# A first batch split by halves of j over all four pieces, and q = 0 copies on ScalarE, in a Fourier-mixing and MLP kernel

## The chip, the cores and the metric

The kernel runs on one core of a Trainium2 chip. The core has five engines, each with its own stream of instructions in a fixed order: TensorE (PE in the profile, with its weight loads listed apart as PEld), VectorE (DVE), ScalarE (ACT), GpSimd (POOL) and SyncE (SP, which only issues DMAs). Instructions on different engines wait for each other through semaphores. DMAs move data between DRAM and the on-chip memory SBUF; matmul results stand in a small memory called PSUM, from which ACT and DVE read.

The metric is the device time of one execution in microseconds (us), less is better. Times are medians of several executions. The profile is of one execution of its own.

## What is computed

The input is `x` of 8 x 4224 x 192 (batch, position, channel), a table of 8 x 7 taps, and two weight matrices. First comes a causal depthwise convolution over positions, with taps that went through a softmax; each of 8 groups of 24 channels has its own 7 taps. Then the real part of a two-dimensional Fourier transform over positions and channels is added to the signal, the sum is normalised, goes through a two-layer MLP, and is added again:

```python
w = np.exp(w); w = w / (np.sum(w, axis=-1, keepdims=True) + 1e-09)
out = np.einsum('hk,bskhg->bshg', w, x_unf)            # 7 taps, 8 groups
...
X = np.fft.fft(np.fft.fft(x, axis=1), axis=2)
u = x + np.real(X).astype(np.float32)
un = (u - mu) / np.sqrt(var + 1e-06)
ch = np.maximum(un @ w_ch1, 0.0) @ w_ch2               # 192 -> 768 -> 192
return (u + ch).astype(np.float32)
```

## The kernel before

**Stages of one batch.** Numbers with L are line numbers.

- *conv.* `conv_unit` loads nothing itself: windows of x (`xt`, from `load_windows`) are multiplied with a band matrix of taps on PE (L387), copied to `xa`, and stored to a scratch in DRAM, `sc`. Six chunks to a batch.
- *load and split.* `load_x` reads the rows back from `sc` in another layout, in four pieces of the index b (`PIECES`: 9, 8, 8 and 8 wide), into `xs` tiles. `split_x` writes each value as a sum of two float16 numbers, so that float16 matmuls keep nearly float32 accuracy: ACT writes the high part `XH` (L472), DVE the remainder `XL` (L473). A piece is split in two halves of b, so there are eight calls of each to a batch.
- *stage A.* `stage_a` has 16 tiles, each with some of the indices j, which go over the short transforms' columns. A tile's matmuls (L490) read the columns of XH and XL for its own j, and all b. The PSUM tile `pa` is split again: ACT writes `yh` (L498), DVE `yl` (L499).
- *stage B.* `stage_b` runs 8 times to a batch (L516 on PE, then ACT L524 and DVE L525 write `V`). At the end of each, POOL copies the q = 0 part of `V` to `V0` (L531), 2 x 6 x 8 values to a partition. V0 is read only by the ninth iteration of the batch, called `Q0`.
- *iterations.* Eight iterations of 512 positions each, and Q0 with 128. For each, POOL gathers the convolved rows into `xr` with indirect DMAs (`load_res`, L544, four to an iteration). `prep` does the last transform on PE (`pq`, L574), ACT moves it to `u` (L591), POOL adds `xr` (L592), DVE takes the statistics, small operations on ACT, DVE and POOL follow, then the normalised rows `un` (DVE or ACT, L623 and L628), and their two float16 parts in `hl` (ACT L638, POOL L641). `transposes` turns `hl` into `kt` with a transposing DMA on SP (L651). `mlp_hidden` (PE `ph` L680, ACT `hh` L684, DVE `hlo` L685) and `mlp_out` (PE `po` L699 to L705, DVE L711) are the MLP; then `u` is stored.

**Order.** The source is written in the order of priority. The scheduler of the language simulates the engines and orders each engine's instructions from that, and an `issue_after(...)` holds an instruction back in that order until another one has been issued. A tile with a `tag` takes one of the `bufs` buffers of that tag; a new tile waits for all readers of the one that had its buffer. Tags are shared between purposes whose lives do not overlap. In the first batch, `xs` pieces 0 and 1 are in the tag `xs` and pieces 2 and 3 in `yh` and `yl`, and the raw words of the second weight matrix (`raw_w2`, two tiles) are in `hlo`, which later holds the low part of the hidden layer.

**The start.** The first batch has nothing to run beside it. It is written out by hand before the main loop: windows, conv, `scales`, four `load_x`, eight `split_x` (L819 to L822), the conversion of the MLP's weights, 16 `stage_a`, then the gathers of iterations 0 and 1, two `stage_b`, the preparation of these two iterations at high priority, then the gathers of iterations 2 and 3 behind `lower[0]`, the last POOL instruction that writes `hl` of iteration 1, then the conv of batch 1 and the rest of the first stage B:

```python
    with tc.issue_after(lower[0]):
        for f in gathers(2) + gathers(3):
            f()
```

In the main loop, which has one turn to an iteration, the preparation of iterations 2 to 4 ahead and the conv, split and stages of the next batch are spread between the MLP's matmuls. There `split_x(bt, i)` is called with i from 0 to 7 at places set by `split_at` and `split_1`: two calls, then the loads, then the others.

## Time and profile before

| | us |
|---|---|
| median of the runs (3) | 1337.24 |
| lowest and highest of them | 1334.99, 1337.45 |
| the profiled execution, its own time | 1339.74 |
| span of that execution's profile | 1338.0 |
| busy time of POOL's gathers, L544, 264 of them | 283.0 |
| busy time of PE in `ph`, L680, 2160 matmuls | 504.0 |
| idle time of PE before L699, put down to ACT `hh` | 34.1 |

The mean granted clock of TensorE over the span was 0.96 of full speed. A busy time is the sum of the durations of an engine's instructions. An idle time before a group of instructions is given with the instruction that ended it, written `<-ACT hh L684`. `<-issue` is idle time in which the engine waited for nothing that the profile shows, and `<-remote` a wait that ended with an event of a queue or a core that it cannot name. In a timeline row stand start, duration, engine, line, operation, output<-inputs, shapes, and how many like it follow; in a row of windows the window, its length, and the busy time with the number of instructions for PE, PEld, DVE, ACT and POOL, then clock, DMA share and GB/s.

### The profile page before, as it was taken

The numbers are of one execution on the slowest core, as the hardware profiler recorded it, in microseconds if no ns is written. First come the engines' busy times: TensorE is split into PE (matmuls) and PEld (weight loads), VectorE is DVE, ScalarE is ACT, GpSimd is POOL, SyncE is SP. The second block draws the span as 40 slices with busy tenths as digits, with TensorE's granted clock in tenths as the row PEclk, the third lists the DMA queues.
The fourth block names the chain that finished last, engine by engine and source line by source line (L and its number), as shares of the span: only waits on it lengthen the run. The fifth ranks groups of instructions, "written<-read, shape, count | busy, mean of one in ns | idle before, by whom it ended". The sixth has DMA issues, their size and how long they took to land.

```text
span 1338.0 us, 30108 instructions
## 1 busy us (share of the span) xinstructions
PE 1204.8 (90%) x12224; PEld 943.1 (70%) x12224; DVE 745.0 (56%) x1635; ACT 819.0 (61%) x1562; POOL 666.5 (50%) x1052
## 2 busy tenths in 40 slices
PE   4186689998999989998999989999889998999999
PEld 4175458885777767786778857777567876777767
DVE  7763365456545565456644575446654566555443
ACT  4643387558755686557865586556755667545642
POOL 0236535457445664457444574456634576456520
PEclk9588889998999999999999999999899999999999
DMA  8934395556555566456554576555564444223321
GB/s 274 241 90 125 90 246 142 104 132 166 132 124 128 126 149 144 121 129 167 120 139 103 122 178 127 128 125 129 141 137 108 116 96 95 69 63 84 75 63 39
DMA packets 225819, 170.19 MB, mean 127 GB/s; under 512 B 119560, under 2 KB 207440, under 8 KB 225680
## 3 DMA queue, kind: packets, MB, share of 16 engines
q1 hardware_dynamic: 163408, 108.53, 35.4%
q10 hardware_dynamic: 49600, 33.77, 10.0%
q0 software_dynamic: 12672, 25.97, 7.5%
q8 instruction: 95, 1.56, 0.5%
q14 instruction: 44, 0.36, 0.1%
HBM read 83.73 MB, written 58.55 MB: 106 GB/s over the span
## 4 chain that ended last, share of the span: by engine, by line
PE 35%; POOL 24%; issue 17%; ACT 11%; DVE 5%; DMA 4%; another core or an unknown queue 1%; SPq 1%; ACTq 0%; POOLq 0%; DVEq 0%
PE ph L680 12%; POOL xr L544 11%; PE pa L490 5%; ACT un L628 4%; POOL u L592 4%; PE po L699 4%; PE po L705 4%; PE po L702 4%; POOL hl L641 4%; DMA xs<-sc 3%; PE pc L387 3%; DVE XL L473 2%; PE pq L574 2%; ACT hl L638 2%; ACT hh L684 1%
## 5 line engine op out<-in xcount | busy, mean ns | idle before, releaser
L680 PE MATMUL ph<-kt,W 128*128 128x512 f16 (+1 forms) x2160 | 504.0, 367 | 18.5 <-DMA kt<-hl 8.4
L685 DVE SCALAR_TENSOR_TENSOR hlo<-ph,hh 128x512 f16<-128x512 f32 (+1 forms) x400 | 270.8, 679 | 346.5 <-ACT hh L684 342.0
L699 PE MATMUL po<-W,hh 128*128 128x192 f16 x1584 | 387.9, 248 | 45.7 <-ACT hh L684 34.1
L702 PE MATMUL po<-W,hh 128*128 128x192 f16 x1584 | 387.9, 248 | 1.3 <-issue 1.3
L705 PE MATMUL po<-W,hlo 128*128 128x192 f16 x1584 | 384.1, 247 | 1.8 <-issue 1.5
L684 ACT ACTIVATE hh<-ph 128x512 f16<-128x512 f32 (+1 forms) x400 | 236.5, 593 | 199.2 <-PE ph L680 141.3
L544 POOL DMA_INDIRECT xr<-sc,rows_sb x264 | 283.0, 1072 | 134.4 <-issue 60.7
L680 PEld LDWEIGHTS <-W 128*128 128x128 f16 x2160 | 196.4, 99 | 170.7 <-issue 25.7
L641 POOL TENSOR_TENSOR hl<-un,hl 128x512 f16<-128x512 f32 (+1 forms) x144 | 129.4, 920 | 219.0 <-ACT hl L638 210.4
L699 PEld LDWEIGHTS <-hh 128*128 128x128 f16 x1584 | 155.8, 98 | 58.9 <-ACT hh L684 38.6
L592 POOL TENSOR_TENSOR u<-u,xr 128x768 f32<-128x768 f32 (+1 forms) x72 | 121.1, 1682 | 129.9 <-ACT u L591 129.7
L702 PEld LDWEIGHTS <-hh 128*128 128x128 f16 x1584 | 155.8, 98 | 28.7 <-issue 14.1
L705 PEld LDWEIGHTS <-hlo 128*128 128x128 f16 x1584 | 155.6, 98 | 27.5 <-issue 5.8
L628 ACT ACTIVATE un<-u,nm,y 128x192 f32<-128x192 f32 x256 | 120.2, 539 | 53.9 <-POOL nm L618 49.5
L387 PE MATMUL pc<-xt,band 128*120 128x144 f32 x756 | 120.5, 301 | 24.2 <-DMA band<-line_d 15.0
L387 PEld LDWEIGHTS pc<-xt,band 128*120 128x120 f32 x756 | 107.3, 193 | 32.6 <-issue 16.1
L490 PE MATMUL pa<-c_sb,XH 128*128 128x128 f16 x1024 | 103.2, 223 | 22.2 <-ACT XH L472 19.1
L711 DVE SCALAR_TENSOR_TENSOR u<-po,fo,u 128x384 f32<-128x384 f32 (+1 forms) x136 | 81.4, 599 | 62.1 <-PE po L705 46.7
L473 DVE SCALAR_TENSOR_TENSOR XL<-xs,s_x,XH 128x768 f16<-128x768 f32 x64 | 104.2, 1638 | 17.1 <-ACT XH L472 10.3
L499 DVE SCALAR_TENSOR_TENSOR yl<-pa,yh 99x512 f16<-99x512 f32 x128 | 85.3, 682 | 49.1 <-ACT yh L498 45.7
L472 ACT ACTIVATE XH<-xs,s_x 128x768 f16<-128x768 f32 x64 | 106.3, 1694 | 7.9 <-DMA xs<-sc 7.9
L490 PEld LDWEIGHTS <-XH 128*128 128x128 f16 x1024 | 82.6, 99 | 32.6 <-ACT XH L472 19.7
(125 smaller groups left out, 1461.5 us busy)
## 6 DMA issues: line engine op xcount, KB each, us to landing
out_dram<-u SPq DMA_DIRECT2D x64, 384.0 KB
xt<-in_xw_dram SPq DMA_DIRECT2D x42, 576.0 KB
sc<-xa ACTq DMA_DIRECT2D x42, 540.0 KB
xs<-sc SPq DMA_DIRECT2D x96, 192.0 KB
xs<-sc SPq DMA_DIRECT2D x32, 216.0 KB
xr<-sc,rows_sb POOLq DMA_INDIRECT x264
sc<-xa ACTq DMA_DIRECT2D x7, 450.0 KB
xt<-in_xv_dram SPq DMA_DIRECT2D x6, 504.0 KB
```

What stands on the lines that cost most here:

```text
L387: nc.tensor.matmul(pc[:WR, h - h0], band[:, h, :WR], xt[:, :, h * GRP : (h + 1) * GRP], start=True, stop=True,)
L490: nc.tensor.matmul(pa[:, i], x[:, at], F[:, l], start=(n == 0), stop=(n == 2))
L544: nc.gpsimd.indirect_dma_start(bt.xr[it][:, g], None, bt.sc[:S], bass.IndirectOffsetOnAxis(ap=rows_sb[:, col : col + 1], axis=0),)
L592: nc.gpsimd.tensor_tensor(u[:, :ng], u[:, :ng], xr[:, :ng], op=ALU.add)
L628: nc.scalar.activation(un[:, g], u[:, g], AF.Identity, bias=nm[:, g : g + 1], scale=y[:, g : g + 1],)
L641: lower[0] = nc.gpsimd.tensor_tensor(bl[:, :, o : o + n], un[:, :ng, f], hi[:, :, f], op=ALU.subtract).ins
L680: nc.tensor.matmul(ph[:, n], W1[:, w, ht * 128 : (ht + 1) * 128], kt[:, k], start=(i == 0), stop=(i == len(order) - 1),)
L684: anchor[0] = nc.scalar.activation(hh, ph, AF.Relu).ins
L685: nc.vector.scalar_tensor_tensor(hlo, ph, 0.0, hh, op0=ALU.max, op1=ALU.subtract)
L699: nc.tensor.matmul(po[:, g % 2], hh[:, ht, tk], W2[:, ht, 0], start=(ht == 0), stop=False)
L702: nc.tensor.matmul(po[:, g % 2], hh[:, ht, tk], W2[:, ht, 1], start=False, stop=False)
L705: nc.tensor.matmul(po[:, g % 2], hlo[:, ht, tk], W2[:, ht, 0], start=False, stop=(ht == 5),)
```

## The change

There are five edits; what is computed stays the same.

1. **Split by j.** `split_x` takes half of the j of a whole piece (9 or 8 wide in b), where it took all j of half a piece. For the first batch, the first halves of all four pieces come first, then the second halves. In later batches the calls keep their places, so the two halves of one piece follow each other.
2. **Slots at the start.** Pieces 2 and 3 of the first batch's `xs` go to the tag `hlo` instead of `yh` and `yl`, and the raw words of the second weight matrix to `xa` instead of `hlo`.
3. **Copies of q = 0.** The copy from `V` to `V0` is an activation on ACT instead of a copy on POOL.
4. **Buffers.** `xr` has 4 buffers instead of 3 and `un` 2 instead of 1.
5. **Gathers at the start.** Those of iterations 2 and 3 follow those of 0 and 1 directly; the `issue_after(lower[0])` goes.

```diff
-        tag, bufs = (("yh", 1), ("yl", 1))[i - 2] if b == 0 and i > 1 else ("xs", 2)
-        xs = sb.tile([NA, 9, D], F32, tag=tag, name=f"xs_{b}_{i}", bufs=bufs)
+        tag, bufs, n = ("hlo", 2, 8) if b == 0 and i > 1 else ("xs", 2, 9)
+        xs = sb.tile([NA, n, D], F32, tag=tag, name=f"xs_{b}_{i}", bufs=bufs)
...
-                raw(f"w2_{i}", "hlo")[:, : 6 * D].rearrange("p (c e) -> p c e", c=3),
+                raw(f"w2_{i}", "xa", 3 * D)[:, : 6 * D].rearrange("p (c e) -> p c e", c=3),
...
-        first = PIECES[i][0]
-        b0, b1 = ((first, first + 4), (first + 4, PIECES[i][1]))[half]
-        src = bt.xs[i][:, b0 - first : b1 - first].rearrange("p b (t j) -> p j (b t)", t=ND)
+        b0, b1 = PIECES[i]
+        js = slice(half * NJ // 2, (half + 1) * NJ // 2)
+        src = bt.xs[i][:, : b1 - b0].rearrange("p b (t j) -> p j (b t)", t=ND)[:, js]
...
-                :, :, ND * b0 : ND * b1
+                :, js, ND * b0 : ND * b1
...
-    for i in range(2 * NPC):
-        split_x(first, i)
+    for half in range(2):
+        for i in range(NPC):
+            split_x(first, 2 * i + half)
...
-        nc.gpsimd.tensor_copy(
+        nc.scalar.activation(
             bt.V0.rearrange("p l m c -> p (l m) c")[:, :, it * CG : (it + 1) * CG],
             V.rearrange("p l (m q) c -> p (l m) q c", q=NQ)[:, :, 0],
+            AF.Copy,
         )
...
-            bt.xr[it] = sb.tile([128, 4, D], F32, tag="xr", name=f"xr_{b}_{it}", bufs=3)
+            bt.xr[it] = sb.tile([128, 4, D], F32, tag="xr", name=f"xr_{b}_{it}", bufs=4)
...
-        un = sb.tile([128, 4, D], F32, tag="un", name=f"un_{b}_{it}", bufs=1)
+        un = sb.tile([128, 4, D], F32, tag="un", name=f"un_{b}_{it}", bufs=2)
...
-    for f in gathers(0) + gathers(1):
+    for f in gathers(0) + gathers(1) + gathers(2) + gathers(3):
         f()
...
-    with tc.issue_after(lower[0]):
-        for f in gathers(2) + gathers(3):
-            f()
```

More of the change, by code (lines that the diff above doesn't have):

```diff
@@ L37 @@
 PIECES = ((0, 9), (9, 17), (17, 25), (25, 33))
+NPC = len(PIECES)
 DUP = 9 * WR
@@ L227, in tmp @@
         def tmp(i):
-            t = sb.tile([128, HID], F32, tag=("kt", "hl", "un")[i], name=f"cv{i}_{name}", bufs=(3, 2, 1)[i])
+            t = sb.tile([128, HID], F32, tag=("kt", "hl", "un")[i], name=f"cv{i}_{name}", bufs=(3, 2, 2)[i])
             return t[:rows, :n]
@@ L249, with raw @@
     raws = {}
-    def raw(name, tag):
-        raws[name] = sb.tile([128, HID, 2], I32, tag=tag, name=f"raw_{name}")
+    def raw(name, tag, n=HID):
+        raws[name] = sb.tile([128, n, 2], I32, tag=tag, name=f"raw_{name}")
         return raws[name].rearrange("p n t -> p (n t)")
@@ L733 @@
     NT = NJ // JT
-    NPC = len(PIECES)
     NIT = NPAIR + 1
```

## The prediction

> **What bounds the kernel now.** I began with the page: span, busy line and the row of the granted clock.
>
> ```profile
> span 1338.0 us, 30108 instructions
> PE 1204.8 (90%) x12224; PEld 943.1 (70%) x12224; DVE 745.0 (56%) x1635; ACT 819.0 (61%) x1562; POOL 666.5 (50%) x1052
> PEclk9588889998999999999999999999899999999999
> ```
>
> TensorE (PE) is 90% busy and no other engine is over 61%. The clock is below full in the first slices only, so the start differs from the rest. The view of windows shows by how much (columns: window, its length, busy time and instructions of PE, PEld, DVE, ACT, POOL, clock, DMA share, GB/s):
>
> ```profile
> 0.00:60.00 60.00, 16.22 (x102) 15.77 (x102) 43.74 (x100) 30.45 (x47) 2.90 (x6) 0.79 0.95 274
> 60.00:100.00 40.00, 32.11 (x378) 30.19 (x379) 28.18 (x62) 23.00 (x43) 15.88 (x27) 0.80 0.33 93
> 100.00:124.00 24.00, 13.32 (x144) 9.70 (x142) 7.43 (x15) 8.11 (x16) 15.32 (x21) 0.78 0.58 150
> 124.00:160.00 36.00, 31.08 (x263) 24.36 (x262) 17.68 (x55) 12.40 (x29) 20.87 (x37) 0.87 0.26 74
> 160.00:180.00 20.00, 8.97 (x37) 5.48 (x38) 6.70 (x6) 14.48 (x19) 7.37 (x6) 0.77 0.91 210
> 200.00:1338.00 1138.00, 1084.98 (x11137) 843.76 (x11134) 627.18 (x1377) 712.03 (x1382) 598.43 (x948) 0.99 0.51 118
> ```
>
> From 200 us on PE is busy 1085.0 of 1138 us: it is the bound, and only 53 us are idle. Before, it idles 10.7 us in 100 to 124 (24 less 13.32), 4.9 in 124 to 160 and 11.0 in 160 to 180. Work that PE can start earlier there ends the program earlier, one for one. Nearly all of the change acts there; only the copies for q = 0 act in every batch. Three rows of PE's timeline show what it waits for:
>
> ```profile
> 61.64 1.03 PE L490 MATMUL pa<-c_sb,XH 128*128 128x128 f16 x8 [18.48 <-ACT XH L472]
> 123.32 0.34 PE L699 MATMUL po<-W,hh 128*128 128x192 f16 x1 [7.15 <-ACT hh L684]
> 166.89 4.33 PE L680 MATMUL ph<-kt,W 128*128 128x512 f16 x10 [8.09 <-DMA kt<-hl]
> ```
>
> These are stage A waiting for the split, the second matmul of iteration 0 waiting for ACT, and iteration 2, whose transposed input arrives late.
>
> **The split by halves of j.** Rows of ACT and DVE around stage A of the first batch:
>
> ```profile
> 48.58 3.55 ACT L472 ACTIVATE XH<-xs,s_x 128x768 f16<-128x768 f32 x2 [6.25 <-DMA xs<-sc]
> 52.13 9.46 ACT L472 ACTIVATE XH<-xs,s_x 128x768 f16<-128x768 f32 x6
> 62.83 1.15 ACT L343 ACTIVATE sq<-xt 128x1152 bf16<-128x1152 f32 x1
> 60.35 2.95 DVE L473 SCALAR_TENSOR_TENSOR XL<-xs,s_x,XH 128x768 f16<-128x768 f32 x2
> 63.24 1.52 DVE L313 SCALAR_TENSOR_TENSOR W<-w,s_w,W 128x576 f16<-128x576 f32 x2
> 65.87 0.69 DVE L499 SCALAR_TENSOR_TENSOR yl<-pa,yh 99x512 f16<-99x512 f32 x1 [1.11 <-ACT yh L498]
> 70.93 7.69 DVE L499 SCALAR_TENSOR_TENSOR yl<-pa,yh 99x512 f16<-99x512 f32 x12 [0.51 <-ACT yh L498]
> ```
>
> Two rows of all later splits say that the cost goes by elements:
>
> ```profile
> L472 ACT ACTIVATE XH<-xs,s_x 128x768 f16<-128x768 f32 x42 | 68.0, 1645 | 0.0
> L472 ACT ACTIVATE XH<-xs,s_x 128x960 f16<-128x960 f32 x6 | 12.2, 2031 | 0.0
> ```
>
> 1645/768 and 2031/960 are both 2.1 ns. Halves of 864 for the first piece and 768 for the others have the same sum as now, so the splits cost nothing more, in later batches too. What changes is that four splits, not eight, release seven of the sixteen tiles of stage A: PE can start near 57 us, not 63. But the four `pa` buffers let it run only four tiles ahead, and ACT and DVE still have the other four splits and W2 before the first `yh` and `yl`. DVE is free at 63.24 + 1.52 = 64.8 us; sixteen `yl` of 0.64 (7.69/12) then end at 75.0 where they end at 78.6 now: 3.6 us at best. ACT has sixteen `yh` and four squares of 1.35 (L343 and its read) in the same stretch, some 13.7 us from 62.8: 76.6 and a gain of 2.0. I take **2.5 us**. That pieces 2 and 3 go to `hlo` frees `yh` and `yl` for this start. Two windows of batch 1 that reuse `xs` now wait for both halves of pieces 0 and 1, some 3 us more; they are used after 88 us, which hides it.
>
> The lower end is in the w2 loads. They move from `hlo` to `xa` slots, so to after the stores of `xa`, beside the loads of `xs`.
>
> ```profile
> raw_w<-in_w_dram ACTq DMA_DIRECT2D x2, 576.0 KB
> DMA packets 5563, 4.07 MB, mean 255 GB/s; under 512 B 270, under 2 KB 5562, under 8 KB 5562
> ```
>
> The second row is the window 34 to 50 us, where 255 GB/s is all that is moved. 1152 KB there are up to 4.6 us in which `xs` could come later. Against that, the same bytes leave the time ahead of the stores, where the DMA share is 0.95 too, so the stores end earlier; I take nothing, bound +4.6. DVE's conversions of w2 fall into its gap of 6.85 us before the first XL.
>
> The Trainium skill (TensorE: Matmul & The Clock Gate, Part 1: The HAM clock gate) says that after an idle window of about 3.4 us the array is back at half rate. By that rule PE, starting at 57 and then waiting for the first `yl`, would run the next 3.4 us at half rate, and the 2.5 would be 0.8. No run here shows this order yet.
>
> **Gathers 2 and 3 and the copies leave POOL's path.** POOL's rows:
>
> ```profile
> 68.40 0.95 POOL L544 DMA_INDIRECT xr<-sc,rows_sb  x1 [0.31 <-issue]
> 104.84 1.08 POOL L544 DMA_INDIRECT xr<-sc,rows_sb  x1
> 118.90 0.95 POOL L544 DMA_INDIRECT xr<-sc,rows_sb  x1 [0.31 <-issue]
> 123.45 0.27 POOL L531 COPY V<-V 128x96 f16<-128x96 f16 x1 [3.12 <-DVE V L525]
> 123.68 1.81 POOL L592 TENSOR_TENSOR u<-u,xr 128x768 f32<-128x768 f32 x1
> 103.10 1.22 ACT L591 ACTIVATE u<-pq,g 128x384 f32<-128x384 f32 x3 [0.29 <-PE pq L574]
> ```
>
> `u` of iteration 2 is ready from ACT at 104.3 us, but POOL adds `xr` at 123.68: before it stand twelve gathers (104.84 to 119.85) and four copies, the last of which waits for V. After the change eight of the gathers follow the first eight directly: 69.4 plus 8 x 1.25 (issue to issue) is 79.4 us. The adds of iterations 0 and 1, which start at 83.64 now and near 81 then, stay clear of them by 1.7 us, and DMA share in 60 to 100 is 0.33. The addition for iteration 2 can come near 106. Its statistics, `un` and transpose follow, and the 8.09 us in which PE waits for its `kt` go; these I count whole, **8 us**. What is late next is the window that conv waits for at 176.93; that 4.1 us wait stays in the sum. With `un` doubled, this row's wait (and one like it at 167.75) goes too:
>
> ```profile
> 163.12 1.86 ACT L628 ACTIVATE un<-u,nm,y 128x192 f32<-128x192 f32 x4 [1.89 <-POOL hl L641]
> ```
>
> It lies in the same late chain, so it adds nothing. Bounds: 0 (something else is late) to 12.2.
>
> **The stall of 108 to 122 us.**
>
> ```profile
> 113.81 0.51 ACT L524 ACTIVATE V<-pb 128x408 f16<-128x408 f32 x1 [5.34 <-remote]
> 122.26 0.51 ACT L524 ACTIVATE V<-pb 128x408 f16<-128x408 f32 x1 [7.95 <-remote]
> 122.81 0.58 DVE L525 SCALAR_TENSOR_TENSOR V<-pb,V 128x408 f16<-128x408 f32 x1 [7.88 <-ACT V L524]
> ```
>
> ACT waits 13.3 us for something the trace cannot name, PE idles 10.7, and both waits lie inside the run of twelve gathers. A run of eight, 57 to 69.4, had no such stall. So I know the place and not the cause. If the stall goes with the eight gathers of twelve, it is 7.1 us; I take half, **3.5 us**. Bounds: 10.7 gained, or 7.1 lost if it goes with them into stage A.
>
> **The clock.** Two waits of PE that should shrink (before 123 and before 166.9) are followed by slow rows:
>
> ```profile
> 124.00:126.00 2.00, 2.00 (x10) 2.00 (x10) 1.04 (x2) 2.00 (x5) 1.49 (x1) 0.50 0.01 4
> 168.00:170.00 2.00, 2.00 (x6) 0.75 (x5) 0.00 (x0) 2.00 (x5) 0.00 (x0) 0.50 1.08 203
> ```
>
> Some 4 us at half rate after each are 2 us lost each. I count one: **2 us** (0 to 4).
>
> **The copies on ACT.** The operation is not in the trace on ACT; the nearest rows bound it.
>
> ```profile
> L531 POOL COPY V<-V 128x96 f16<-128x96 f16 x64 | 17.9, 281 | 94.6 <-DVE V L525 94.5
> L610 ACT ACTIVATE sd<-mv,eps 128x4 f32<-128x4 f32 x64 | 19.0, 296 | 57.7 <-DVE mv L599 52.4 <-DVE hlo L685 3.5 <-issue 1.1
> L638 ACT ACTIVATE hl<-un 128x192 f16<-128x192 f32 x8 | 2.9, 361 | 0.2
> PE po L699 <- ACT hh L684: 26.4, 19, 2.9
> ```
>
> 4 columns take 296 ns and 192 take 361, so 96 take some 0.33 us. Fifty-six of the 64 lie after 200 us. A copy must also wait for DVE's V: ACT ends its half at 122.77, DVE at 123.39, so ACT stands up to 0.62 us unless other work is put between. At most 0.95 us each, 53 in all. Behind a waiting copy stand `hh` (L684) on ACT, and PE's `po` behind that. The last row counts that wait from 200 us on: 19 times, among 379 `hh` activations, 5%. By that share 53 us of ACT cost PE 2.7; with copies put where V is already there, 18.5 us cost 0.9. I take **2 us lost**. Upper end: ACT is busy 712 of 1138 us, 63%, and if PE lost that share of 53 it would be 33. POOL loses 64 x 0.28 us of work and 94.5 us of waiting, but after 200 us PE waits for no `kt`, so that gains nothing; below zero I allow 1.
>
> **Sum.** -2.5 - 8 - 3.5 - 2 + 2 = -14. The profiled execution took 1339.74 us (span 1338.0 and 1.7 around it), 2.5 over the median of the runs, 1337.24. With the median as base: **1323 us**.
>
> **Rivals.**
> - *The stall goes along* (0.18). Sixteen gathers in one run, 57 to 79.4, stand beside the whole of stage A. For: both long waits lie in such runs. Against: the first run of eight. Where the stall only moves, stage A's 2.5 is lost with it: 1337.2 - 8 - 2 + 2 = 1329; where it also grows by its 7.1 there, 1336. I take 1330.
> - *xs comes later* (0.10). The w2 loads delay the first split by 4.6 us: 1328. Beside it: the Trainium skill (DMA: Bandwidth & Descriptors, Queues, rings and completion order) has each engine take turns between the queues it has work for; by that rule w2 on ACT's queue would take a share from `xs` on SP's, which speaks against this part of the change.
> - *Nothing is left of it* (0.11). Iteration 2 comes earlier, but PE then waits where it is idle next, for batch 1's windows and `xs`, DMA-bound at a share of 0.91 in 160 to 180 us: only stage A and what the copies cost remain, 1337. That is also what is left if the halves don't release PE, as four `pa` buffers allow little.
> - *ACT becomes late* (0.16), the other side. Each copy holds ACT until DVE's V, `hh` comes late, PE idles. With the start gaining 16, it decides from 16/56 = 0.29 us of PE per copy. Half of the bound, 0.5 us each, is 28 us: 1349; at the bound of 33, 1354.
> - The forecast, 1323, has 0.45.
>
> **How the numbers follow.** All gains at their ends (3.6, 12.2, 10.7, 4, 1) would give 1306. The range leaves out the last of that and most of the case in which ACT is late: 1309 to 1343. About 0.2% is what a measurement of this kernel can tell from no change (1334.6 to 1339.9). Faster: 0.45, nearly all of the first two rivals (0.24) and a little of the third: 0.72. Same: most of the third and the edge of the first: 0.12. Slower: the last, 0.16.
>
> **What would show it.** Stage A: the first `pa` matmul with XL near 57 us and the last `yl` near 76. Gathers: sixteen between 57 and 80 us, and the add for iteration 2 near 106. PE: the window 160 to 180 busy 17 us or more, not 9. The stall: no wait of ACT's V over 2 us. ACT: the wait of `po` for `hh` from 200 us on still near 26 us. I am wrong if that wait is over 40, if the stall stands at another place with its full length, or if the hole before iteration 2 only moves.

## The result and the profile after

The changed kernel takes **1346.17 us** (median of 5 runs, 1342.87 to 1348.13). The kernel before takes 1337.45 us on the same chip (5 runs). The ratio is **1.0061**, 95% interval 1.004 to 1.0081: slower by 0.6%. The forecast was 1323 us, with a range up to 1343.

The page of the changed kernel, whose profiled execution took 1348.13 us (span, busy line, granted clock):

```profile
span 1346.2 us, 30076 instructions
PE 1209.6 (90%) x12224; PEld 944.1 (70%) x12224; DVE 746.0 (55%) x1635; ACT 830.3 (62%) x1626; POOL 641.5 (48%) x988
PEclk9577899998999989999899989999999998999999
```

POOL has 25 us less work and ACT 11 more, but PE is busy 4.8 us longer for the same 12224 matmuls, and the span is 8.2 us longer. The view of windows (columns as before) shows the start:

```profile
60.00:100.00 40.00, 25.70 (x292) 22.12 (x293) 21.00 (x37) 21.27 (x41) 17.38 (x17) 0.71 0.27 89
100.00:124.00 24.00, 16.41 (x142) 15.44 (x141) 13.86 (x41) 7.06 (x17) 17.20 (x29) 0.72 0.64 177
124.00:160.00 36.00, 28.85 (x271) 21.89 (x269) 18.70 (x57) 20.51 (x46) 20.88 (x32) 0.93 0.79 176
160.00:180.00 20.00, 17.40 (x147) 13.88 (x146) 10.54 (x12) 16.10 (x25) 4.62 (x8) 0.95 1.02 221
200.00:1346.20 1146.20, 1089.19 (x11122) 844.38 (x11119) 625.08 (x1373) 720.78 (x1432) 570.58 (x886) 0.98 0.50 117
```

The hole of 160 to 180 us is gone: PE is busy 17.4 there, not 9. But 86 matmuls are missing from 60 to 100 us. One mark helps to divide the program: the start of the n-th hidden activation (`hh`, one to each group of `ph`, 50 to a batch), read from the trace of both kernels. All numbers in this table are such starts, counted from the first instruction.

| `hh` number | before, us | changed, us | difference |
|---|---|---|---|
| 0 | 106.3 | 126.2 | +19.9 |
| 12 | 169.5 | 171.2 | +1.7 |
| 48 (end of batch 0) | 284.0 | 282.4 | -1.6 |
| 99 | 441.1 | 442.5 | +1.3 |
| 249 | 907.1 | 914.6 | +7.6 |
| 399 (last) | 1330.2 | 1338.5 | +8.2 |

So there are **two results, not one**. The start gains 1.6 us, where 16 were forecast. And from `hh` 48 on the changed kernel loses 9.8 us, where the copies were forecast to cost 2. Inside a batch the loss stands at one place: in each batch from the second to the fifth the difference grows by 1.9 to 2.8 us, nearly all of it between the hidden units 4 and 22, mostly in iterations 1 and 2. Behind them it departs by up to 1.2 us at single units and comes back.

For the start, rows of ACT, DVE and POOL in the timeline of the changed kernel:

```profile
72.46 0.60 ACT L499 ACTIVATE yh<-pa 99x512 f16<-99x512 f32 x1 [1.81 <-PE pa L491]
83.78 0.60 ACT L499 ACTIVATE yh<-pa 99x512 f16<-99x512 f32 x1 [10.73 <-remote]
90.38 3.67 DVE L500 SCALAR_TENSOR_TENSOR yl<-pa,yh 99x512 f16<-99x512 f32 x6
81.53 0.94 POOL L546 DMA_INDIRECT xr<-sc,rows_sb  x1 [0.30 <-issue]
99.43 1.81 POOL L594 TENSOR_TENSOR u<-u,xr 128x768 f32<-128x768 f32 x1 [16.96 <-ACT u L593]
113.81 0.21 POOL L617 TENSOR_TENSOR t<-t,w 128x4 f32<-128x4 f32 x1
123.80 1.81 POOL L594 TENSOR_TENSOR u<-u,xr 128x768 f32<-128x768 f32 x1 [1.05 <-ACT u L593]
```

The wait that the trace cannot name (the stall), seen before at 108 to 122 us, now stands in stage A: 10.7 us of ACT before 83.78, beside the run of sixteen gathers that ends at 82.5. The last `yl` ends at 94.1, not 76. Then the addition for iteration 0 (99.43) and a later small step of its chain on POOL (`t`, L617, 113.81) lie 14 us apart, because eight more gathers, of iterations 4 and 5, went between them (101.5 to 113.8): the fourth `xr` buffer let them through. The addition for iteration 2, which was to move from 123.7 to 106, stays at 123.8; it waits there for `u` from ACT.

### The profile page after: what moved, and what is told of

Same layout as the page of the kernel before. It is cut to its first block, busy times and chain, and to the rows that moved or that the text cites. A ratio compares the mean times of both kernels' runs of the same rounds, so it can differ in the third digit from the quotient of the medians.

```text
span 1346.2 us, 30076 instructions
## 1 busy us (share of the span) xinstructions
PE 1209.6 (90%) x12224; PEld 944.1 (70%) x12224; DVE 746.0 (55%) x1635; ACT 830.3 (62%) x1626; POOL 641.5 (48%) x988
## 4 chain that ended last, share of the span: by engine, by line
PE 38%; POOL 18%; issue 15%; ACT 10%; DMA 9%; DVE 6%; SPq 1%; ACTq 1%; POOLq 0%; DVEq 0%
PE ph L682 14%; POOL xr L546 9%; PE po L707 4%; PE po L701 4%; PE po L704 4%; POOL u L594 4%; PE pa L491 4%; ACT un L630 4%; DMA out_dram<-u 3%; PE pc L388 3%; PE pq L576 3%; POOL hl L643 2%; ACT hh L686 2%; DVE XL L474 2%; DMA xs<-sc 2%
## 5 line engine op out<-in xcount | busy, mean ns | idle before, releaser
L546 POOL DMA_INDIRECT xr<-sc,rows_sb x264 | 278.8, 1056 | 138.5 <-DMA xt<-in_xw_dram 60.7
L704 PEld LDWEIGHTS <-hh 128*128 128x128 f16 x1584 | 155.8, 98 | 21.4 <-issue 6.8
L491 PE MATMUL pa<-c_sb,XH 128*128 128x128 f16 x1024 | 109.6, 227 | 39.8 <-ACT XH L473 29.2
L388 PE MATMUL pc<-xt,band 128*120 128x144 f32 x756 | 118.2, 297 | 28.2 <-DMA band<-line_d 14.9
L388 PEld LDWEIGHTS pc<-xt,band 128*120 128x120 f32 x756 | 105.7, 190 | 38.4 <-issue 16.7
L491 PEld LDWEIGHTS <-XH 128*128 128x128 f16 x1024 | 85.4, 101 | 51.2 <-ACT XH L473 29.3
L474 DVE SCALAR_TENSOR_TENSOR XL<-xs,s_x,XH 128x768 f16<-128x768 f32 (+1 forms) x64 | 101.2, 1590 | 25.1 <-ACT XH L473 24.9
L499 ACT ACTIVATE yh<-pa 99x512 f16<-99x512 f32 x128 | 74.7, 599 | 64.7 <-PE pa L491 25.1
```

The lines of the kernel that those rows point to most:

```text
L388: nc.tensor.matmul(pc[:WR, h - h0], band[:, h, :WR], xt[:, :, h * GRP : (h + 1) * GRP], start=True, stop=True,)
L491: nc.tensor.matmul(pa[:, i], x[:, at], F[:, l], start=(n == 0), stop=(n == 2))
L546: nc.gpsimd.indirect_dma_start(bt.xr[it][:, g], None, bt.sc[:S], bass.IndirectOffsetOnAxis(ap=rows_sb[:, col : col + 1], axis=0),)
L704: nc.tensor.matmul(po[:, g % 2], hh[:, ht, tk], W2[:, ht, 1], start=False, stop=False)
```

## The experiments

A ratio is against the kernel before on the same chip, with its 95% interval. The series ran on more than one chip: the kernel before took 1337 to 1339 us in the first three series and 1314 in the last two, so only ratios compare across them. Where a batch's length is given, it is the mean distance from `hh` 50n to `hh` 50(n+1) over the second to the fifth batch, in the one profiled execution; for the kernel before it is 155.3 us, for the changed one 157.6.

### Each part undone

Copies back on POOL:

```diff
-        nc.scalar.activation(V0 slice, V slice, AF.Copy)
+        nc.gpsimd.tensor_copy(V0 slice, V slice)
```

> The changed kernel with the q = 0 copies back on GpSimd, all else as changed. From 210 us to the end the changed kernel loses 10.4 us on the kernel before (its 24th hh is 2.6 us earlier, its last 7.9 later). Copies theory: these 10 us are ACT waiting for DVE's V at the copies, so this run takes 1336 us, 10 below the changed kernel. Buffers theory (second un) and split theory (halves of j): the copies cost the 2 us that I forecast, 1344. Either way the first hh stays near 126 us.

Measured: 1330.91 us, 0.9956 (0.9943 to 0.997). This is faster than both kernels, by 15 us against the changed one. A batch takes 155.3 us again. The first `hh` stays at 126.1. In the profiles it beats the kernel before by 4.7 us up to `hh` 48 and by 4.0 after it, and the 4.0 come from one batch that is not in the means: `hh` 250 to 300 takes 158.1 us here, 163.0 before and 162.4 in the changed kernel.

The halves of b again, in every batch:

```diff
-        b0, b1 = PIECES[i]
-        js = slice(half * NJ // 2, (half + 1) * NJ // 2)
+        first = PIECES[i][0]
+        b0, b1 = ((first, first + 4), (first + 4, PIECES[i][1]))[half]
...
-    for half in range(2):
-        for i in range(NPC):
-            split_x(first, 2 * i + half)
+    for i in range(2 * NPC):
+        split_x(first, i)
```

> The changed kernel with the split by halves of b again, in every batch and in the old order for the first; slots, copies, buffers and gathers stay as changed. The loss of each later batch, 2.0 to 2.4 us, falls in its iterations 1 and 2, where the next batch is split. Split theory: that loss goes with the halves of j, 1336 us. Buffers and copies theories: 1346 within 2, and the loss per batch stays. At the start the halves of j released stage A at 60.6 us where it was 61.6, so undoing them costs 1 us at most.

Measured: 1356.83 us, 1.0143 (1.0125 to 1.0161). The split theory falls: undoing the halves of j does not remove the loss of the later batches (158.6 us each). It costs 10.7 us, so beside the other edits the halves of j are worth that much, about half of it at the start (`hh` 48 at 287.3 instead of 282.4) and 1.0 us in each later batch.

One `un` buffer (the temporary of the weights' conversion that has the same tag goes back to one with it):

```diff
-        un = sb.tile([128, 4, D], F32, tag="un", name=f"un_{b}_{it}", bufs=2)
+        un = sb.tile([128, 4, D], F32, tag="un", name=f"un_{b}_{it}", bufs=1)
```

> The changed kernel with one un buffer instead of two (and one of the conversion's temporaries with it), all else as changed. Buffers theory: with two, ACT takes the four un of an iteration ahead of an hh and then stands waiting for POOL's nm (3.1 us at 471.8 to 474.8 us of the changed kernel, hh behind it, PE idle 2.1), so the 10 us go: 1336. Copies and split theories: 1346, or up to 3 more for the waits of un that come back.

Measured: 1341.53 us, 1.0033 (1.002 to 1.0046). A batch takes 156.3 us, between the two. The second buffer does harm here, but it doesn't make up the whole loss.

Gathers of iterations 2 and 3 late again:

```diff
-    for f in gathers(0) + gathers(1) + gathers(2) + gathers(3):
+    for f in gathers(0) + gathers(1):
         f()
...
+    with tc.issue_after(lower[0]):
+        for f in gathers(2) + gathers(3):
+            f()
```

> The changed kernel with the gathers of iterations 2 and 3 behind the last hl of iteration 1 again, all else as changed. Theory of the moved stall: the run of sixteen gathers, 61 to 82.5 us, is what holds PE in stage A at one instruction in 0.7 us from 69.2 to 84.9; with eight gathers the yl end near 80 and the first hh comes near 107 instead of 126. The hole before iteration 2 returns (8 us), so the time is within 4 us of the changed kernel's 1346. Rival: stage A is slow for another reason (W2's conversion on DVE, four pa buffers): the gaps of 1.0 to 1.15 us in stage A stay, and the first hh stays past 120.

Measured: 1362.43 us, 1.0191 (1.0175 to 1.0206). In stage A the theory of the moved stall held: with eight gathers (60 to 73 us) only 2.5 us of waits without a name are left there, and the last `yl` ends at 84.1. The first `hh` comes 9.6 us earlier, at 116.6, but not near 107, as the first transpose took 12.4 us from issue. The time was far off the 1346 within 4 us. With four `xr` buffers the late gathers run into those of iterations 4 and 5, a run of sixteen from 105.9 to 125.9 us with 10.3 us of that wait in it, and `hh` 48 comes 17.5 us later than in the changed kernel. The early gathers are worth that.

### The copies and the second buffer

Copies on POOL and one `un` buffer; and the kernel before with nothing but the copies on ACT:

> Copies back on GpSimd and one un buffer. With the copies on ACT one buffer was 4.6 us faster than two (1341.5 against 1346.2). If the second buffer by itself lets un stand ahead of hh on ACT, the same comes off again: 1326. If it only did harm together with the copies, 1331 within 2, or slower by the waits of un on hl (1.9 us each at 163 and 168 us of the kernel before).

> The kernel before with the q = 0 copies on ACT and nothing else of the change. Copies theory: they cost 15.3 us in the changed kernel (1346.2 less 1330.9), spread over the batches at 1.8 each, whatever else is there: 1352 within 4. Rival, an interaction with two un buffers: 1340 or less, about the 2 us that I forecast. Rival, chance of the order that the scheduler finds: no even slope, but steps at single iterations.

Measured: 1337.99 us, 0.9986 (0.9973 to 1.0), and 1339.41 us, 0.9999 (0.9987 to 1.0011). In both the main theory was wrong and a rival held, and together they say what the first four runs could not. The copies alone cost nothing in the time. Beside the rest of the change they cost 0.5% with one buffer (1.0033 against 0.9986) and 1.05% with two (1.0061 against 0.9956), and the second buffer without them is a gain of 0.3%. The lengths of a batch show the same:

| a batch, us | one `un` | two `un` |
|---|---|---|
| copies on POOL | 156.0 | 155.3 |
| copies on ACT | 156.3 | 157.6 |
| copies on ACT, in the kernel before | 155.8 | |

With one buffer a batch loses 0.3 us by the copies (0.5 in the kernel before, which is within the spread of its four batches, 155.1 to 156.4). With two it loses 2.3. The groups of ACT in the changed kernel and in the kernel before with the copies alone (times busy, mean, idle before it):

```profile
L532 ACT ACTIVATE V<-V 128x96 f16<-128x96 f16 x64 | 17.9, 280 | 16.5 <-DVE V L526 15.9 <-DVE XL L474 0.5
```

```profile
L531 ACT ACTIVATE V<-V 128x96 f16<-128x96 f16 x64 | 18.0, 282 | 17.5 <-DVE V L525 17.5
```

The 64 copies hold ACT for 34 to 36 us in both. In the first they make a batch 2.3 us longer, in the second 0.5. So the price isn't in the time that ACT gives to them.

To see which copies do it, they were divided:

```diff
+        if it < 5:      # and, in the second run, it >= 5
+            nc.scalar.activation(to, q0, AF.Copy)
+        else:
+            nc.gpsimd.tensor_copy(to, q0)
```

> The changed kernel with the copies of stage B 0 to 4 on ACT and those of 5 to 7 on POOL. In the changed kernel the loss of each batch falls in its iterations 1 and 2 (hidden units 6 to 18), the copies of stage B 0 to 4 of the next batch fall elsewhere, and there no hh moves by more than 0.2 us. Theory: the loss hangs on what stands on ACT and POOL at iterations 1 and 2, so without those three copies it goes whole: 0.994 to 0.998 of the kernel before, as with all copies on POOL (0.9956). Rival, an even price of each copy (15 us over 64): 5.7 us less than the changed kernel, 1.002. Rival, a chance order: no rule, anywhere from 0.995 to 1.008.

> The other way round: copies of stage B 5 to 7 on ACT, 0 to 4 on POOL. Theory: the whole loss stays, 1.006 of the kernel before with 2.0 to 2.4 us lost in iterations 1 and 2 of each batch. Rival, an even price: 9.5 us less than the changed kernel, 0.999. Rival, a chance order: anywhere from 0.995 to 1.008, and then this run and the one with 0 to 4 do not add up to the changed kernel.

Measured: 1336.22 us, 1.0001 (0.9986 to 1.0015), with a batch of 155.1 us; and 1350.6 us, 1.0095 (1.0077 to 1.0113), with a batch of 157.4. In the batches the theory held: the loss hangs on the three copies of stage B 5 to 7, which fall in iterations 0 and 1, and the other five cost nothing there. Neither time came out as expected, because the start moved too, with no edit there but those copies: `hh` 48 at 283.7 and 291.8, against 279.2 with all copies on POOL. Batch 0 moves by several us with each such edit; no run explains that part.

One suspect for the later batches is an order that can be read off ACT's timeline. In the changed kernel:

```profile
468.98 0.60 ACT L686 ACTIVATE hh<-ph 128x512 f16<-128x512 f32 x1 [0.98 <-PE ph L682]
469.47 1.62 ACT L473 ACTIVATE XH<-xs,s_x 128x768 f16<-128x768 f32 x1
471.45 0.30 ACT L612 ACTIVATE sd<-mv,eps 128x4 f32<-128x4 f32 x1 [0.36 <-DVE mv L601]
474.81 1.86 ACT L630 ACTIVATE un<-u,nm,y 128x192 f32<-128x192 f32 x4 [3.06 <-POOL nm L620]
476.57 0.57 ACT L686 ACTIVATE hh<-ph 128x512 f16<-128x512 f32 x1
```

With the copies on POOL, the same place:

```profile
463.45 0.60 ACT L685 ACTIVATE hh<-ph 128x512 f16<-128x512 f32 x1 [0.97 <-PE ph L681]
463.94 1.61 ACT L473 ACTIVATE XH<-xs,s_x 128x768 f16<-128x768 f32 x1
465.45 0.29 ACT L611 ACTIVATE sd<-mv,eps 128x4 f32<-128x4 f32 x1
465.64 0.58 ACT L685 ACTIVATE hh<-ph 128x512 f16<-128x512 f32 x1
466.11 1.63 ACT L473 ACTIVATE XH<-xs,s_x 128x768 f16<-128x768 f32 x1
469.64 3.61 ACT L629 ACTIVATE un<-u,nm,y 128x192 f32<-128x192 f32 x8 [1.90 <-POOL nm L619]
```

In the first, the four `un` stand ahead of an `hh` and a split. ACT waits 3.1 us for POOL's `nm`, and the `hh` for which PE waits stands behind it. In the second, `hh` and the split come first. It looks like the cause, but two things speak against it. The run with one `un` buffer and the copies on ACT, whose batch takes 156.3 us, has the same order and the same wait:

```profile
475.95 1.86 ACT L630 ACTIVATE un<-u,nm,y 128x192 f32<-128x192 f32 x4 [3.08 <-POOL nm L620]
```

And the next wait of PE for an `hh` is shorter in the changed kernel than with the copies on POOL:

```profile
477.20 0.26 PE L701 MATMUL po<-W,hh 128*128 128x192 f16 x1 [2.10 <-ACT hh L686]
473.79 0.34 PE L700 MATMUL po<-W,hh 128*128 128x192 f16 x1 [3.12 <-ACT hh L685]
```

What does differ is PE's idle time as a whole and the time at half clock (means of the same four batches):

| a batch, us | length | PE idle | clock at 0.50 |
|---|---|---|---|
| one `un`, copies on POOL | 156.0 | 7.85 | 2.6 |
| one `un`, copies on ACT | 156.3 | 8.87 | 0.9 |
| two `un`, copies on POOL | 155.3 | 6.85 | 5.1 |
| two `un`, copies on ACT | 157.6 | 8.10 | 6.8 |

The copies add 1.0 us of idle time with one buffer and 1.25 with two, nearly the same. But the time at half clock falls by 1.7 us with one and rises by 1.7 with two. Matmuls take twice as long there (those of `pa` in the changed kernel start 0.11 us apart up to 66.3 us and 0.06 after), so as an estimate that is 0.85 us off and 0.85 on. Together this gives 0.2 and 2.1 us, where 0.3 and 2.3 were measured. So most of what separates the two pairs is the clock in the profiled executions. Which of the longer waits brings the half clock, and whether other executions of these kernels have the same stretches, is not shown.

### The start

The first sixteen gathers replaced by plain loads; the gathers spread in time; only those of iterations 4 to 7 held back. All three have the copies on POOL.

```diff
+        if b == 0 and it < 4:
+            r0 = 128 * (4 * it + g)
+            nc.sync.dma_start(bt.xr[it][:, g], bt.sc[r0 : r0 + 128])
+            return
```

> Copies back on GpSimd (as the run that takes 1330.9), and the residual rows of iterations 0 to 3 of the first batch come by sixteen plain loads on SyncE's queue, of 128 neighbouring rows each, instead of sixteen gathers; they are other rows, so the output of these four iterations differs, and the bytes are the same. Gather theory: what holds PE in stage A is POOL's gathers themselves; without them the gaps over 0.45 us in stage A, 13.3 us of 70 to 92, fall below 2 and the last yl is near 78 instead of 93. Rival (DMA traffic or the reads of XH): the bytes still move, the gaps stay above 8 us.

```diff
+    def after(src):
+        return nc.gpsimd.tensor_copy(seen[:, :1], src).ins
...
+    with tc.issue_after(after(first.yl[:1, 0, 0, 31:32])):
+        for f in gathers(1):
+            f()
...
+        with tc.issue_after(added[0]):
+            for f in gathers(2 + k):
+                f()
...
+        if b == 0 and 3 < it < Q0 and g == 0:
+            bt.held = after(bt.h[it - 4][0][:1, 0, :1])
```

> Copies back on GpSimd, and the gathers at the start spread: four, then four after a yl of stage A's middle, four after each of the first two additions of xr, and those of iterations 4 to 7 each after the first hh of the iteration four before; a copy of one element on POOL makes each wait. Theories: a run of over six gathers slows PE until 2 us after its end, and gathers of iterations 4 and 5, let through by the fourth xr buffer, stand on POOL ahead of the small operations of iterations 0 and 1 (the t of iteration 0 comes at 114 us, 14 after its addition). If both hold, no gap over 1 us is left in stage A, the first hh comes near 105 instead of 126, and the time falls by 5 to 15 from 1330.9. If only the first holds, hh near 115 and 3 to 5; if the start is bound by its transfers, the first hh is earlier and the 18th is not, 1331.

The third keeps only the last of these edits:

> Copies on POOL and the sixteen gathers in one run as in the changed kernel; only the gathers of iterations 4 to 7 wait, each for the first hh of the iteration four before. It divides the start between its two theories. Second theory (gathers let through by the fourth xr buffer stand ahead of iteration 0's small operations): the t of iteration 0 follows its addition within 5 us, the first hh comes near 114 instead of 126, and the time is 1 to 3 us over the run with spread gathers, 0.992. If that theory carries nothing and the stall of stage A all, 0.9956 as with the copies on POOL alone. Stage A keeps its gaps of 13 us.

Measured: 1328.44 us (one run; the kernel before 1339.4); 1326.92 us, 0.9908 (0.9892 to 0.9924); and 1338.46 us, 1.0004 (0.9991 to 1.0016). ACT's waits from 60 to 100 us, first with all sixteen gathers (copies on POOL), then with plain loads:

```profile
ACT yh L499 <- remote: 12.9, 3, 9.5
ACT V L525 <- PE pb L517: 1.7, 1, 1.7
```

```profile
ACT sd L615 <- DVE mv L604: 2.9, 1, 2.9
ACT yh L499 <- PE pa L491: 2.5, 3, 1.5
ACT V L525 <- PE pb L517: 1.7, 1, 1.7
```

The gather theory held: without gathers, and with the gathers spread, the wait without a name is gone from the start, though the bytes still move. Stage A, from the first matmul of `pa` to the last `yl`, then takes 20 and 23 us, against 34 with all sixteen gathers. Later the spread kernel has a run of nine gathers, 179 to 192 us, and there the wait is back:

```profile
193.20 1.57 ACT L499 ACTIVATE yh<-pa 99x512 f16<-99x512 f32 x3 [5.43 <-remote]
```

With plain loads the first `hh` stays at 127.2, for the other reason: the gathers of iterations 4 and 5 (94 to 104 us) stand between iteration 0's addition (90.5) and its `t` (105.6), those of iteration 6 (114 to 119) stand ahead of POOL's `hl` (119.0), and PE waits 9.1 us for the transpose before its first `ph`.

With only the gathers of 4 to 7 held, `t` (105.7) comes 5.2 us after the addition ends, nearly as expected, but the first `hh` at 123.8, not 114, since PE waits for the transposed rows:

```profile
121.52 4.42 PE L685 MATMUL ph<-kt,W 128*128 128x512 f16 x10 [5.66 <-DMA kt<-hl]
```

With both edits it comes at 115.7. But in both kernels the first half of `hl` is complete at 111.0 us; the difference is the transpose. It takes 10.5 us from issue with the gathers only held, with a DMA share of 1.02, and 3.4 us with both edits, with a share of 0.57. The 12.4 us in the run with late gathers went with a share of 1.00. That the fuller DMA engines slow it is likely and not shown. Holding alone made the kernel slower, not faster: 1.0004 against 0.9956 with the copies on POOL, and `hh` 48 at 287.7 instead of 279.2. And the first `hh` of the spread kernel stands where the first theory alone was to put it, near 115: there the gathers of iterations 2 and 3 stand between iteration 0's addition and its `t`, 12.9 us. So the gain in the time is shown for the run of gathers in stage A, and not for the gathers ahead of the small operations.

The old slots, in the kernel with spread gathers:

```diff
-        tag, bufs, n = ("hlo", 2, 8) if b == 0 and i > 1 else ("xs", 2, 9)
+        tag, bufs = (("yh", 1), ("yl", 1))[i - 2] if b == 0 and i > 1 else ("xs", 2)
+        n = 9
...
-                raw(f"w2_{i}", "xa", 3 * D)[:, : 6 * D].rearrange("p (c e) -> p c e", c=3),
+                raw(f"w2_{i}", "hlo")[:, : 6 * D].rearrange("p (c e) -> p c e", c=3),
```

> The run with spread gathers (0.9908 of the kernel before) with the old slots: pieces 2 and 3 of xs in the buffers of yh and yl, the words of w2 in hlo. There stage A's PE runs from 59.4 to 80.6 us, against 61.6 to 77.3 before, although its stall is gone. Theory: the late w2 puts DVE's conversions and squares of W2 between the splits and the yl; with the old slots they come before the first split again, and stage A ends by 77. Against it, the halves of j can no longer release stage A, since yh and yl are free only after the second halves: the start is near 62. Sum: 0.988 to 0.991. Rival: the slots carry the gain of the halves; without them 0.993 or more.

Measured: 1330.28 us, 0.9949 (0.9931 to 0.9967). PE's last matmul of stage A ends at 74.7 us instead of 80.6, as the theory of W2 says (its last conversions on DVE run at 61.5 us instead of 75.7), and PE even starts earlier, at 58.5. The sum was still worse by 0.4%, as the rival had it: by `hh` 48 the slots as changed are 4 us ahead. The early end of stage A is not what counts there.

### Other chips

The kernel before with spread gathers and nothing else; a quarter of the rows in the first sixteen gathers (with a clearing of `xr` on DVE, and the copies on POOL); the gathers spread further:

```diff
-        for f in gathers(2) + gathers(3):
+        for f in gathers(2):
             f()
...
+    with tc.issue_after(added[0]):
+        for f in gathers(3):
+            f()
```

> The kernel before, and of the change nothing; only its gathers are spread: those of iteration 2 stay behind the last hl of iteration 1, those of 3 follow the addition of iteration 2, those of 4 to 7 each the first hh of the iteration four before. Runs of 12 (105 to 120 us) and 8 (131 to 141) become runs of 4 and at most 8. If a run of over six gathers is what slows PE, the waits of ACT's V put down to no known engine (5.3 and 8.0 us) and PE's gaps of 7.2 and 1.5 us go, the addition of iteration 2 comes near 112 instead of 123.7, and the time is 8 to 15 us lower: 0.989 to 0.994 of the kernel before. Rival: the stall is something else of that place (xt loads, conv of batch 1), gaps and time stay within 3 us.

```diff
-            bt.xr[it][:, g], None, bt.sc[:S],
+            bt.xr[it][:n, g], None, bt.sc[:S],     # n = 32 for b == 0 and it < 4
```

> Copies on POOL and all gathers as in the changed kernel, but each of the first sixteen brings 32 rows instead of 128; the other 96 rows of xr are zero, so the output of the first four iterations differs. If PE is slowed by the count of gather instructions in a run, the gaps in stage A stay (13 us over 0.45 between 70 and 92) and begin after some six gathers. If it is by the rows (descriptors, bytes) that are moved or written, a quarter of them in each, the gaps begin later or not at all: sum below 4 us, last yl near 80.

> The run with spread gathers, further spread: those of iteration 3 wait for the last hl of iteration 1 (in that run they and those of iteration 2 were one run of eight, 91 to 103 us), and Q0's gather waits as those of 4 to 7 do. PE's gaps of 1.0 and 1.1 us near 107 to 109 go. What it costs: the addition of iteration 3 may come later. Expected within 3 us of that run's 1326.9: the gaps left there are small, and the longest ones (5.3 before conv, 3.9 before po) wait for a window and for hh, not in a run of gathers.

Measured: 1308.83 us, 0.9957 (0.9942 to 0.9972); 1321.26 us (one run); 1308.78 us, 0.9962 (0.9947 to 0.9978). But the kernel before took 1313.96 us in this series. To compare, the kernel with the copies on POOL, the quarter of the rows and the spread gathers were run together again:

> The kernel with the copies back on POOL again, beside the next two on one chip, since the run with a quarter of the rows was on another chip (the kernel before took 1314 us there, 1337 elsewhere). Expected 0.9956 of the kernel before, as the first time, and 13 us of gaps over 0.45 in stage A between 68 and 92 us. If the stall belongs to the chip and not to the kernel, the gaps differ from that here.

> The run with a quarter of the rows in the first sixteen gathers, now on one chip with its counterpart of whole rows. If the rows that a gather moves make the stall, the gaps in stage A over 0.45 us sum to less than half of the counterpart's (it was 5.5 us with whole rows not run there); if the count of gather instructions does, they are alike.

> The run with spread gathers again, for its ratio on another chip: 0.9908 the first time, while the further spread one came to 0.9962 where the kernel before took 1314 us. If the spread gains the same everywhere, 0.989 to 0.993; if it gains by the stall alone and that is smaller on a faster chip, 0.994 to 0.997.

Measured, beside 1314.14 us: 1309.54 us, 0.9963 (0.9949 to 0.9976); 1320.78 us (one run); 1312.18 us, 0.9985 (0.9974 to 0.9996). Stage A in the same program, copies on POOL, on the first chip and on the last (windows):

```profile
60.00:69.00 9.00, 7.75 (x87) 7.49 (x88) 8.59 (x12) 5.96 (x10) 6.85 (x4) 0.61 0.63 244
69.00:85.00 16.00, 5.02 (x45) 2.78 (x42) 2.93 (x9) 4.08 (x10) 11.32 (x12) 0.65 0.30 81
```

```profile
60.00:69.00 9.00, 7.91 (x92) 7.52 (x93) 8.44 (x12) 5.90 (x11) 7.10 (x5) 0.66 0.67 258
69.00:81.00 12.00, 7.24 (x112) 6.28 (x109) 9.57 (x20) 10.90 (x21) 9.26 (x10) 1.00 0.28 76
```

Both run their sixteen gathers, to 83.7 and 84 us, with the same DMA share. Up to 69 us they are alike. Then PE starts 45 matmuls in 16 us on the first chip and 112 in 12 us on the last. The first `hh` comes at 112.7 instead of 126.1. In all six profiles of the last two series, on two chips, no wait of ACT or DVE is `<-remote`, however the gathers stand. The spread gathers' run of nine comes there too (176 to 188 us), without a wait. In the earlier profiles, between 55 and 165 us, only the runs with plain loads and with spread gathers are free of it; with spread gathers and old slots it is 0.9 us, in the other nine, the changed kernel and the kernel before 8 to 21. So the stall needs two things: a run of gathers, and the chip, or something else that differed between those series.

It is not all of the 23 us between the chips. With the copies on POOL, `hh` 48 comes 14.2 us earlier on the last chip, and the rest of the program is 7.3 us shorter, 153.7 instead of 155.3 us a batch; the cause of that part is open.

The runs with a quarter of the rows say nothing about rows or count, since there was no stall to divide. What is slower in them is the start, where POOL's order differs: in the second of them eight gathers in one run (93.8 to 103.6 us) and four more (113.3 to 118.2) stand ahead of the first `hl`, which is complete at 120.0 us instead of 106.7. The spread gathers fell short of both their expected ranges on the last chip (0.9985), and the kernel before with spread gathers alone came to 0.9957, where 0.989 to 0.994 was expected.

## Why the prediction was wrong, step by step

1. **Stage A, 2.5 us gained: wrong, 15.5 lost.** The last `yl` ends at 94.1 us, not 76. The halves of j released PE at 60.6, not 57, as the scheduler's order on ACT is both halves of one piece, then both of the next, and not the four first halves. W2's conversions, which were to fall into DVE's gap before the first XL, ended between the `yl`. Most of it is the moved stall. Beside the loss to half rate that was weighed there, the Trainium skill (TensorE: Matmul & The Clock Gate, Part 1: The HAM clock gate) has the array back at full rate after at least one busy window of about 3.4 us. The granted clock stayed at 0.50 until 66.3 us, 5.8 after the first matmul, so the slow stretch was longer than the 3.4 us reckoned; before, it lasted from 61.6 to 68.6, so the change lost nothing by it.
2. **Iteration 2 earlier, 8 us: the hole went, the gain did not come.** PE is busy 17.4 us in 160 to 180, as forecast. But the addition did not move, since iterations 0 and 1 themselves came 20 us later and the hole closed from the other side. The step that failed is "after the change eight of the gathers follow the first eight directly": it didn't count the next eight. With a fourth `xr` buffer those of iterations 4 and 5 find a buffer as soon as iteration 0 has added, and take POOL ahead of its small operations. Held and spread, the change came to 0.9908; held alone, to 1.0004. So what the run of sixteen costs is shown; of the next eight it is shown that they delay iteration 0's `t` and `hl`, and not what that costs in the end.
3. **The stall, 3.5 us gained: wrong side.** It moved with the gathers into stage A and grew: the same program has its first `hh` 13.4 us later on the chip with the stall than on the one without. This was the rival "the stall goes along", with a chance of 0.18 and a growth in stage A of up to 7.1 us, about half of that.
4. **The clock, 2 us gained:** wrong side too. From `hh` 48 on PE's idle time grew by 3.8 us (windows from 282 us: 1056.0 less 1003.15, and 1064.2 less 1007.53) and its busy time by 4.4 for nearly the same matmuls. In the trace the stretches at half rate after 212 us sum to 43.0 us, before to 35.8. At half rate that is, as an estimate, some 3.6 us of work, so the loss shows half as waits and half as clock.
5. **The copies, 2 us lost: mis-sized.** After `hh` 48 the changed kernel takes 1056.1 us, with the copies on POOL 1042.3: 13.8 us. The bounds held it (-1 to 33). The step that failed is the price by ACT's time per copy, in the forecast and in the rival "ACT becomes late" alike. The same 34 to 36 us of ACT cost 0.5 us a batch in the kernel before and 2.3 beside a second `un` buffer, through three of the eight copies. Nor does the rival's mechanism, PE idle for a late `hh`, show: from 282 us on, first in the changed kernel and then with the copies on POOL,

```profile
PE po L701 <- ACT hh L686: 28.0, 27, 2.7
PE ph L682 <- DVE hlo L687: 15.4, 26, 2.2
PE po L701 <- DVE u L713: 4.3, 4, 1.4
```

```profile
PE po L700 <- ACT hh L685: 29.0, 23, 3.2
PE ph L681 <- DVE hlo L686: 10.6, 17, 1.8
PE po L700 <- DVE u L712: 0.6, 2, 0.4
```

The waits for `hh` did not grow; those for DVE did. Of the 13.8 us, 7.6 are idle time of PE, and as an estimate some 5 are clock (43.0 us at half rate after 212 us, against 32.0). What makes DVE late stays open. Besides, "only the copies for q = 0 act in every batch" left out the second `un` buffer and the halves of j, which moved a later batch by 0.7 (155.3 against 156.0) and 1.0 us in the runs; the buffer had been put at nothing ("it adds nothing").
6. **w2 beside `xs`, up to 4.6 us later: did not come.** The first split starts at 47.91 us, before at 48.58.

The wait of `po` for `hh` from 200 us on is 28.0 us (26.4 before), as the forecast asked for. I had said I would be wrong over 40. (The second sign came true: the stall stands at another place, with more than its length.) That first test was badly chosen: the loss showed in `ph`, which waits 15.4 us for `hlo` where it was 6.7 before, and in the clock.

The steadiest of the versions that ran is the change with its copies left on POOL: 0.9956 and 0.9963 of the kernel before on two chips. With the gathers spread it was 0.9908, the lowest of all, on a chip with the stall and 0.9985 on one without. On such chips the kernel before with spread gathers and nothing else (0.9957) is as good as four of the five edits.

## What to carry to other kernels

Where a scheduler orders the engines, an edit is not priced by the time it takes on its engine: two edits of which one is free and the other a gain can cost together, so the runs must cross them in pairs. An order on one engine that looks like the cause must be looked for in the kernels that don't lose, too. A buffer added to a pool is not only a wait less; it lets work through ahead of something else on an in-order queue, and one must list what. And a wait that a trace cannot name may belong to the chip: before building on it, run the same program on a second one.

## What the runs showed of the hardware

Runs of gathers on POOL can hold TensorE. In the changed kernel on its chip, PE fell to one matmul in about 0.7 us from 70 to 85 us (22 recorded), with gaps of 1.0 to 1.15 us that are put down to `issue` and a DMA share of 0.27. It began some 10 us after the first gather of the run and ended 2.7 us after the last.

The 14 profiles of the first series, up to the run with old slots, have 83 gaps of PE over 0.85 us with `issue` as their end. Every one lies inside a run of gathers or at most 3 us behind it, though such stretches are only 0.4 of the span. Most belong to runs of eight or more. Runs of four show one gap of 0.9 to 1.1 us here and there, in five of the kernels, and in four kernels ACT waits 2.5 to 3.9 us without a name at a run of four. With plain loads of the same bytes stage A has none.

On the two other chips, where the kernel before is 23 us faster, the six profiles have no such gap at all, and two of the programs are the same. What differs, and by which path gathers reach TensorE, stays open.
